# Six pairs of token groups loaded, scaled and scored with two tokens per partition, in a fused retention and gated two-layer kernel

## Chip, cores and metric

The kernel runs on one core of a Trainium2 chip. The metric is the device time of one execution in microseconds. Before the change the median of three runs is 299.77 us (299.62 to 301.11).

## What is computed

Eight batches of 576 tokens, eight heads of 64, give 4608 tokens of width 512. A masked linear attention with a decay per head comes first; a two-layer product with g = h cos(h) between the layers follows. Inputs and output are float32.

```
scores = (1/8) * q @ k.T                      # per batch and head, 576 x 576
Dmat   = where(i >= j, gamma[h] ** (i - j), 0)
attn   = (scores * Dmat) @ v
x      = attn with heads side by side          # 4608 x 512
h      = x @ w_in                              # 512 -> 2048
out    = (h * cos(h)) @ w_out                  # 2048 -> 512
```

## The kernel before

**Tiling.** The 4608 tokens are 36 groups of 128, numbered 0 to 35. Nine groups make two batches (`PER` = 9), and a group with g % 9 == 4 (`MIX`: 4, 13, 22, 31) lies across the end of a batch. The decay is split into a factor on q and a factor on k, so that each group needs only a 0/1 mask on its own 128 x 128 scores, and the earlier groups of the batch come in through a carried state of 64 x 64 per head.

**One group's way.** `load` (L105) brings q, k and v in with one DMA each from SP's queue, 128 partitions by 8 heads by 64 floats, in packets of 256 bytes (a token of one head). `prep` (L131) multiplies q and k by their factors into `qks` (L140, on GpSimd, 128 x 512 each) and rounds v to bfloat16 (L156). A group across two batches also copies the second batch's rows into `v_odd` (L158), whose other rows are zero, so that its state takes only these. `transposes` (L164) turns q and k: for groups below 6 on TensorE, with ScalarE copying the result (L177), from group 6 on by a DMA of SP's queue (L167). `scores` (L187) multiplies k by q (L195); VectorE masks the result (L207). `state` (L219, one group, L231) and `states` (L248, two groups, L266) make k.T @ v, and VectorE keeps the running sum (L285, L287) or masks it (L240). `attn_out` (L293) sums the group's own product, scores by v (L333), and the carried one, q by state (L319), and an engine moves it to `xT` (L350).

**Forms on TensorE.** The profile writes a matmul's place in the array as rows*columns. In `scores` with `parts=2` four matmuls of 64*64 use four quarters of the array; in `states` and the own product two matmuls of 128*64 use its two column halves; `attn_out` of two groups has its carried product in 64*64, with four quarters in turn.

**The two-layer part.** Tokens are taken in ten stretches n of widths 512, 256, 256 and seven times 512. `mm1` (L354) makes h (L365), ScalarE the cosine (L373), VectorE the product `gT` (L374). For n = 0 to 2, `mm2` (L376) makes the second product with 16 matmuls per 128 tokens (L382), ScalarE copies it (L392), SP stores it, and `feed(s)` follows. From n = 3 on, `mm2_seven` (L527) uses seven products of quarter matrices (L517) instead of eight; their sums of quarters of g (`g_sum`, L425, L445) are made by GpSimd and VectorE, the sums of quarters of w_out by `w_sums` (L404, L418).

**What sets the order.** The order is written by hand: each engine, and each DMA queue of SP or GpSimd, does its instructions in the order in which the Python program issues them, and waits at an instruction until its inputs are there. For n = 0 to 2, a list `todo` of (index, work) is mixed into the sequence of `mm2` matmuls: the work is issued ahead of the matmul with that index. For n = 0 the 64 matmuls run as `order` (L842 to L848): indices 0 to 31 are tokens 0 to 255, 32 to 47 the third 128 and 48 to 63 the fourth. `feed(s)` is called by `mm2` after the last matmul of each 128 tokens, so after indices 27, 31, 47 and 63. It issues loads, preps and transposes (L599 to L631). By its limits it issues, in this order:

| call | after index | issues |
|---|---|---|
| feed(0) | 27 | load 6, prep 6, load 7, transposes 6 |
| feed(1) | 31 | prep 7, load 8, prep 8, transposes 7, load 9, transposes 8 |
| feed(2) | 47 | prep 9, load 10, prep 10, transposes 9, load 11, transposes 10 |
| feed(3) | 63 | prep 11, load 12, prep 12, transposes 11, load 13, transposes 12 |

Groups 4 and 5 are loaded at L726 and L727, the first gated behind the second part of w_out, and prepared at L739, ahead of all that `feed` issues. Preps up to group 15 are issued in n = 0 to 2, the later ones by n = 3 and on.

Of the kernel before, what the change touches and what calls it, by code (L numbers as in the profile page):

```python
# [17 lines left out]
def kernel(  # L18
# [17 lines left out]
    P = 128  # L36
# [19 lines left out]
    N_PE_T = 6  # L56
    S7 = 3
# [27 lines left out]
    gk = consts.tile([P, PER, H], F32)  # L85
    ln_scale = consts.tile([P, 1], F32)
    half_pi = consts.tile([P, 1], F32)
    tri = consts.tile([P, P], F32)
    tri_mix = consts.tile([P, P], F32)
    diag2 = consts.tile([P, P], F32)  # L90
# [5 lines left out]
    v_odd = consts.tile([P, 2, H, D], BF16)  # L96

# [6 lines left out]

    def load(g, names="qkv", gate=None):  # L105

        t0 = g * P
# [4 lines left out]
        for name in names:  # L112
            src = {"q": q, "k": k, "v": v}[name]
            f = ld.tile([P, H, D], F32, tag="f" + name, name=f"f{name}")
            for p0, p1, t in parts:
                b, s0 = divmod(t, S)
                i = nc.sync.dma_start(  # L117
                    f[p0:p1], src[b, :, s0 : s0 + p1 - p0, :].rearrange("h s d -> s h d")
                )
                if gate is not None:  # L120
                    tc.add_manual_dep(
                        i.ins, gate.ins.name,
                        mybir.DependencyInfo(
                            mybir.DependencyClass.Sync, mybir.DependencyReason.DATA
                        ),
                        reason="weights first",
                    )
                    gate = None
            tiles["f" + name, g] = f

    def prep(g, early=False, kv_first=False):  # L131

        c = g % PER
# [30 lines left out]
    def transposes(g, banks=None, only=(0, 1)):  # L164
        qks, vb, qkT, qT = tiles["a", g]
# [52 lines left out]

    def state(g):  # L219
# [3 lines left out]
        qks, vb, qkT, qT = tiles["a", g]  # L223
# [4 lines left out]
        p0 = HP if c == g == MIX else 0  # L228
        vs = v_odd[:, g // PER % 2] if c == MIX and g > PER else vb
        for hg in range(HG):  # L230
            nc.tensor.matmul(  # L231
                ps[:, hg, :],
                lhsT=qks[p0:, 1, 2 * hg : 2 * hg + 2, :].rearrange("s h d -> s (h d)"),
                rhs=vs[p0:].rearrange("s (a b) d -> s b a d", a=2)[:, hg],
                start=(fresh and hg == 0),
                stop=(c in (MIX - 1, PER - 2) and hg == HG - 1),
                skip_group_check=True,
            )
# [9 lines left out]
    def states(gs, bank="st"):  # L248
# [6 lines left out]
        apart = bank == "b"  # L255
        if apart:
            two = psum.tile([P, 2, 2, HG, D], F32, tag=bank, name="st")
            ps = two[:, :, 0]
        else:
            ps = psum.tile([P, len(gs), HG, D], F32, tag=bank, name="st")  # L260
        for x, g in enumerate(gs):
            qks, vb, qkT, qT = tiles["a", g]
            vs = v_odd[:, g // PER % 2] if g % PER == MIX else vb
            for hg in range(HG):
                for he in range(2):
                    nc.tensor.matmul(  # L266
                        ps[he * D : he * D + D, x, hg, :],
                        lhsT=qks[:, 1, 2 * hg + he, :],
                        rhs=vs[:, head(he, hg), :],
                        start=((apart or x == 0) and hg == 0),  # L270
                        stop=((apart or x + 1 == len(gs)) and hg == HG - 1),
                        skip_group_check=True,
                    )

        def copy(run=nc.vector.tensor_copy):
            for g in gs:
                s, sb = tiles.pop(("s32", g)), blocks4[g % 4]
                run(sb, s)
                tiles["sb", g + 1] = sb

        def add():
            for x, g in enumerate(gs):
                s = stp.tile([P, HG, D], F32, tag="s32", name="s32")
                if g % PER in (0, MIX):
                    nc.vector.tensor_copy(s, ps[:, x])  # L285
                else:
                    nc.vector.tensor_tensor(out=s, in0=ps[:, x], in1=tiles["s32"], op=ALU.add)  # L287
# [361 lines left out]
    for p0, c0, c1, base in (  # L649
# [4 lines left out]
        )  # L654
    nc.gpsimd.memset(tri, 1.0)
# [23 lines left out]
    nc.scalar.activation(gk, pos, ACTF.Exp, bias=0.0, scale=-1.0)  # L679
    nc.vector.memset(v_odd[:HP], 0.0)  # L680
    nc.vector.memset(diag2, 0.0)
# [38 lines left out]
    for g in range(G4):  # L720
# [3 lines left out]
        if g == 2:  # L724
# [4 lines left out]
            nc.gpsimd.memset(tri_mix[:HP, HP:], 0.0)  # L729
        if g + 1 < G4:  # L730
# [8 lines left out]
    for g in (4, 5):  # L739
        prep(g)  # L740
# [3 lines left out]
    def pair(g, banks, sc, av):  # L744

        mid = (sc + av) // 2
        return [
            (sc - 5, lambda: state(g)),
            (sc, lambda: (scores(g, banks[0]), scores(g + 1, banks[1]))),
            (mid, lambda: state(g + 1)),  # L750
            (av, lambda: attn_out([g, g + 1], banks[0])),
        ]

    def scores2(g, put_off=None):
        if g < NG:
# [3 lines left out]
    def unit(g, bank, more=True, soon=False):  # L759

        attn_out([g, g + 1], bank, nc.scalar.copy)
        copy = states([g + 1, g + 2])()
# [7 lines left out]
    def unit7(g, bank, more=True, then=lambda: None, put_off=None):  # L770
# [3 lines left out]
        attn_out([g, g + 1], "m", nc.scalar.copy)  # L774
# [5 lines left out]
    for n, w in enumerate(widths):  # L780
# [6 lines left out]
        elif n == 1:  # L787
            blocks = [(et, half * P, P) for half in range(2) for et in (0, 8)]
# [6 lines left out]
        for i, (et, c0, cw) in enumerate(blocks):  # L795
# [3 lines left out]
                (1, 0): {4: lambda: scores(5, "a")},  # L799
                (1, 1): {3: lambda: attn_out([5], "a", evac=nc.scalar.copy)},  # L800
# [8 lines left out]
        if n == 0:  # L809
            todo = [  # L810
                (34 + 5 * i, lambda x=x, e=e: w_sums(x, e, e + 4))
                for i, (x, e) in enumerate((x, e) for x in (1, 6, 7) for e in (0, 4))
            ] + [
                (45, lambda: transposes(4, "ab")),
                (49, lambda: state(4)),
                (50, lambda: scores(4, "a")),
                (57, lambda: attn_out([4], "a")),
# [66 lines left out]
```

## Time and profile before

| | |
|---|---|
| median of three runs | 299.77 us |
| span of the profiled execution, first to last instruction | 298.2 us |
| TensorE busy | 287.1 us, 3113 matmuls |
| TensorE clock granted, mean | 1.000 |
| VectorE, ScalarE, GpSimd busy | 207.9, 135.9, 209.4 us |
| DMA packets, of these under 512 bytes | 154304, 140832 |
| DMA queue of SP (q1): packets, MB, share of 16 engines | 149504, 45.10, 77.2% |
| n = 0: first layer, second layer begin at | 17.91, 32.79 us |
| n = 1: first layer, second layer begin at | 49.17, 57.61 us |
| n = 2: first layer, second layer begin at | 67.49, 74.47 us |
| n = 3: first layer begins at | 84.18 us |

The span is what the profiler saw of one execution; the time of that execution itself is not among its rows, so the distance of 1.6 us from span to median is used for it. The beginnings are those of the first matmul of L365 or L382 in the order of time on TensorE.

A view in order of time gives start, length, engine, line and operation of each instruction or run of equal instructions, then the idle time ahead of it and what ended that. Matmuls overlap, so that the time from one start to the next is the cost and the length is not.

### The profile page before, as it was taken

Reading aid. Unit: us, or ns where it says so; the run is one execution under the profiler, and the core shown is the slowest. Engines: PE = TensorE matmul, PEld = TensorE weight load, DVE = VectorE, ACT = ScalarE, POOL = GpSimd, SP = SyncE. Lnnn points to the kernel's source line nnn. Section 1 sums busy time; section 2 is a strip of 40 time slices with the busy share of each in tenths; the row PEclk is TensorE's granted clock in tenths of the full one; section 3 lists DMA queues with packets and bytes.
Section 4 is the critical chain, followed back from the end, with each engine's and each line's share of the span. In section 5 each row is a group of like instructions: output and inputs, shape, how many; then the busy total and the mean of one; then the engine's idle time right before and its main releaser. Section 6 shows DMA issues by size and latency. Waiting matters only on the chain.

```text
span 298.2 us, 7384 instructions
## 1 busy us (share of the span) xinstructions
PE 287.1 (96%) x3113; PEld 195.3 (65%) x3113; DVE 207.9 (70%) x245; ACT 135.9 (46%) x167; POOL 209.4 (70%) x214
## 2 busy tenths in 40 slices
PE   8899999999999999979999999999999999999995
PEld 3478646848578786448744875488448845874584
DVE  5677637564579994788848874887489757935872
ACT  2656433514255432642346554546464446425620
POOL 2750066436445599997999999599959946980693
PEclk9999999999999999999999999999999999999999
DMA  7999999999999999999999997998690260031013
GB/s 203 212 209 206 209 214 213 200 243 208 208 174 222 211 239 213 217 279 176 198 224 229 209 200 183 212 208 201 122 194 2 73 143 0 2 106 36 0 44 99
DMA packets 154304, 50.28 MB, mean 169 GB/s; under 512 B 140832, under 2 KB 153248, under 8 KB 154272
## 3 DMA queue, kind: packets, MB, share of 16 engines
q1 hardware_dynamic: 149504, 45.10, 77.2%
q0 software_dynamic: 4224, 4.19, 8.5%
q8 instruction: 24, 0.39, 0.6%
q10 hardware_dynamic: 544, 0.52, 0.5%
q14 instruction: 8, 0.07, 0.1%
HBM read 36.70 MB, written 9.44 MB: 155 GB/s over the span
## 4 chain that ended last, share of the span: by engine, by line
PE 43%; POOL 25%; SPq 13%; DMA 8%; DVE 5%; issue 3%; ACT 1%; POOLq 0%; DVEq 0%
PE h L365 22%; POOL gs L445 17%; PE o L517 11%; SPq L117 8%; POOL qks L140 6%; PE o L382 5%; SPq L167 4%; DVE gT L374 3%; DMA fk<-in_k_dram 2%; DMA w_in_sb<-in_moe_w_in_dram 2%; DMA qkT<-qks 2%; POOL vb L156 2%; DVE gs L445 2%; DMA fv<-in_v_dram 1%; ACT cosh L373 1%
## 5 line engine op out<-in xcount | busy, mean ns | idle before, releaser
L445 POOL TENSOR_TENSOR gs<-gT 128x512 bf16<-128x512 bf16 x102 | 116.3, 1180 | 29.4 <-DVE gs L445 29.4
L365 PE MATMUL h<-xT,w_in_sb 128*128 128x512 bf16 (+2 forms) x832 | 127.6, 313 | 2.6 <-DVE gT L374 1.8
L374 DVE TENSOR_TENSOR gT<-h,cosh 128x1024 bf16<-128x1024 f32 x72 | 87.8, 1223 | 43.7 <-ACT cosh L373 40.7
L373 ACT ACTIVATE cosh<-h,half_pi 128x1024 f32<-128x1024 f32 x72 | 80.2, 1114 | 72.2 <-PE h L365 69.8
L365 PEld LDWEIGHTS <-w_in_sb 128*128 128x128 bf16 x832 | 75.9, 98 | 51.6 <-issue 3.0
L140 POOL TENSOR_TENSOR qks<-fq,gq 128x512 bf16<-128x512 f32 x32 | 34.0, 1062 | 40.9 <-DMA fq<-in_q_dram 40.9
L517 PEld LDWEIGHTS <-gs 128*128 128x128 bf16 x576 | 53.6, 98 | 10.1 <-POOL gs L445 2.9
L140 POOL TENSOR_TENSOR qks<-fk,gk 128x512 bf16<-128x512 f32 x35 | 37.3, 1066 | 8.0 <-DMA fk<-in_k_dram 7.4
L207 DVE TENSOR_TENSOR ret<-sc,tri 128x1024 bf16<-128x1024 f32 x32 | 38.1, 1217 | 2.8 <-PE sc L195 2.7
L517 PE MATMUL o<-ws,gs 128*128 128x256 bf16 (+1 forms) x352 | 39.1, 268 | 0.7 <-POOL gs L445 0.5
L382 PE MATMUL o<-w_out_sb,gT 128*128 128x512 bf16 x128 | 30.1, 380 | 0.0
L517 PE MATMUL o<-w_out_sb,gT 128*128 128x256 bf16 x224 | 26.6, 273 | 0.1
L517 PE MATMUL o<-w_out_sb,gs 128*128 128x256 bf16 x224 | 26.1, 273 | 0.5 <-POOL gs L445 0.4
L537 DVE TENSOR_TENSOR ot<-o,ot 128x512 f32<-128x512 f32 (+2 forms) x25 | 14.9, 603 | 14.7 <-PE o L517 14.5
L517 PEld LDWEIGHTS <-gT 128*128 128x128 bf16 x224 | 21.4, 98 | 4.7 <-DVE gT L374 0.7
L350 ACT CAST xT<-ov 128x1024 bf16<-128x1024 f32 (+1 forms) x18 | 16.5, 917 | 16.1 <-PE ov L319 13.9
L445 DVE TENSOR_TENSOR gs<-gT 128x1024 bf16<-128x1024 bf16 (+1 forms) x18 | 20.4, 1148 | 0.3
L382 PEld LDWEIGHTS <-gT 128*128 128x128 bf16 x128 | 11.8, 98 | 12.5
L156 POOL CAST vb<-fv 128x512 bf16<-128x512 f32 x22 | 14.3, 651 | 4.4 <-DMA fv<-in_v_dram 4.2
L564 ACT COPY ot<-o 128x512 f32<-128x512 f32 x7 | 4.1, 586 | 20.5 <-PE o L517 20.5
L392 ACT COPY ot<-o 128x512 f32<-128x512 f32 x8 | 4.7, 588 | 17.4 <-PE o L382 17.4
L537 DVE TENSOR_TENSOR ot<-ot,o 128x512 f32<-128x512 f32 x14 | 9.6, 684 | 4.0 <-ACT ot L569 2.4
(70 smaller groups left out, 175.8 us busy)
## 6 DMA issues: line engine op xcount, KB each, us to landing
out_dram<-ot SPq DMA_DIRECT2D x35, 256.0 KB, 4.0
fk<-in_k_dram SPq DMA_DIRECT2D x32, 256.0 KB, 5.2
fv<-in_v_dram SPq DMA_DIRECT2D x32, 256.0 KB, 5.2
fq<-in_q_dram SPq DMA_DIRECT2D x30, 256.0 KB, 4.5
w_in_sb<-in_moe_w_in_dram POOLq DMA_DIRECT2D x4, 512.0 KB, 8.9
w_out_sb<-in_moe_w_out_dram POOLq DMA_DIRECT2D x4, 512.0 KB, 16.2
fq<-in_q_dram SPq DMA_DIRECT2D x8, 128.0 KB, 4.0
fk<-in_k_dram SPq DMA_DIRECT2D x8, 128.0 KB, 4.4
```

The lines of the kernel that those rows point to most:

```text
L117: i = nc.sync.dma_start(f[p0:p1], src[b, :, s0 : s0 + p1 - p0, :].rearrange("h s d -> s h d"))
L140: eng.tensor_tensor(out=qks[:, m].rearrange("p (b a) d -> p a b d", a=2), in0=f.rearrange("p (a b) d -> p a b d", a=2), in1=by[:, c, :].re ...
L156: copy_v(vb, fv)
L207: nc.vector.tensor_tensor(out=ret.rearrange("p a b i -> p (a b) i"), in0=ps.rearrange("p a b i -> p (a b) i"), in1=mask.unsqueeze(1).to_br ...
L350: evac(tiles["x", n][:, :, t0 : t0 + len(gs) * P], ps.rearrange("p c x i -> p c (x i)"))
L365: nc.tensor.matmul(ps[:, j, :], lhsT=w_in_sb[:, dg, (et + j) * P : (et + j + 1) * P], rhs=xT[:, dg, c0 : c0 + w], start=(dg == 0), stop=(d ...
L373: nc.scalar.activation(cosh, ps, ACTF.Sin, bias=half_pi, scale=1.0)
L374: nc.vector.tensor_mul(gT[:, et : et + m, c0 : c0 + w], ps, cosh)
L382: nc.tensor.matmul(ps, lhsT=gT[:, et, tsi * P : (tsi + 1) * P], rhs=w_out_sb[:, et, :], start=(et == 0), stop=(et == ET - 1),)
L445: i = (nc.vector if on_dve else nc.gpsimd).tensor_tensor(out=tiles["gs", n, x][:, e : e + step], in0=i0, in1=i1, op=op_)
L517: nc.tensor.matmul(dst[i], lhsT=lhs[:, e, j * P : (j + 1) * P], rhs=rhs[:, e, c0:c1], start=(x in (3, 4, 1, 7) and e == 0 and (i == 0 or l ...
L537: pend.append(lambda: nc.vector.tensor_tensor(out=out_, in0=in0, in1=in1, op=op_))
```

## The change

Groups 4 to 15 become six pairs. A pair's 256 tokens lie two to a partition, the tokens 2i and 2i+1 of the pair in partition i, so that the first group has partitions 0 to 63 and the second 64 to 127. A tile of a load then holds four heads of 256 tokens (`he` is the half of the heads) in packets of 512 bytes. An even group's load brings q of both halves and k of the first, an odd group's brings k of the second and both halves of v. `prep2` does the same thirds on GpSimd. The DMAs and their sizes stay as many as before.

In the scores, own products and states, r (0 or 1) is the token in the partition, x the group in the pair. Of the own products and the states each matmul reads 64 partitions now instead of 128, and there are twice as many. The carried product reads all 128 partitions against a masked 128-column state `sb` instead of 64 against 64. New constants (`gq2`, `gk2`, three masks, `v2_odd`) are made by GpSimd, VectorE and ScalarE in the beginning.

Pair 2 (groups 4 and 5) has a way of its own: at the place of L739 only the first half of the heads of q and k is scaled on GpSimd. The rest is in the new `todo` of n = 0: VectorE scales the second halves at index 30, ScalarE rounds v and GpSimd copies the second batch's rows of v into `v2_odd` (`odd2`) at index 48, ahead of `state(4)` at index 54, whose matmuls read `v2_odd`. Group 5's scores and output, which stood in the first layer of n = 1, are now part of the pair; that layer runs in blocks of 256 tokens instead of 128.

The core of the diff:

```diff
+    PAIRED = range(4, 16)
...
+    def load2(g, gate=None):
...
+        for name, he in (("k", 1), ("v", 0), ("v", 1)) if g % 2 else (("q", 0), ("q", 1), ("k", 0)):
...
+            f = ld.tile([P, HG, 2, D], F32, tag="f" + name, name=f"f{name}")
+            for p0, p1, bb, sa in ((0, pm, b, s0), (pm, P, b + 1, 0)):
+                if p0 < p1:
+                    i = nc.sync.dma_start(
+                        f[p0:p1].rearrange("p h r d -> p h (r d)"),
+                        src[bb, he * HG : he * HG + HG, sa : sa + 2 * (p1 - p0), :].rearrange(
+                            "h (p r) d -> p h (r d)", r=2
+                        ),
+                    )
...
+    def rounded2(p, he, copy):
+
+        f = tiles["fv", p, he]
+        vb = nat.tile([P, HG, 2, D], BF16, tag="vb", name="vb")
+        copy(vb, f)
+        tiles["v2", p, he] = vb
+
+    def odd2(p, he, copy):
+
+        f = tiles.pop(("fv", p, he))
+        for x in mixed2(p):
+            r = slice(x * HP + QH, x * HP + HP)
+            copy(v2_odd[r, he * HG : he * HG + HG], f[r])
+
+    def prep2(g):
+
+        p = g // 2
+        if g % 2 == 0:
+            scaled2("q2", p, 0, nc.gpsimd)
+            scaled2("q2", p, 1, nc.gpsimd)
+            scaled2("k2", p, 0, nc.gpsimd)
+        else:
+            scaled2("k2", p, 1, nc.gpsimd)
+            for he in range(2):
+                rounded2(p, he, nc.gpsimd.tensor_copy)
+                odd2(p, he, nc.gpsimd.tensor_copy)
...
+    def scores_pair(g, banks="ab", put_off=None):
...
+        for r in range(2):
+            ps = psum.tile([P, 2, HG, P], F32, tag=banks[r], name="sc")
+            for hg in range(HG):
+                for x in range(2):
+                    i = slice(x * HP, x * HP + HP)
+                    for he in range(2):
+                        d = slice(he * D, he * D + D)
+                        nc.tensor.matmul(
+                            by_query(ps[i, he, hg, :]),
+                            lhsT=kT[d, r, hg, i],
+                            rhs=qT[d, :, hg, i],
...
+    def attn_pair(g, bank, evac=nc.scalar.copy):
...
+        def out_of(h, x):
+            return ps[h % 2 * D : h % 2 * D + D, x, h // 2, :]
...
+            for h0 in range(0, H, 2):
+                for r in range(2):
+                    for h in (h0, h0 + 1):
+                        for x in range(2):
+                            i = slice(x * HP, x * HP + HP)
+                            nc.tensor.matmul(
+                                out_of(h, x),
+                                lhsT=tiles["v2", p, h // HG][i, h % HG, r, :],
+                                rhs=ret[r][i, h // HG, h % HG, :],
...
+            for hg in range(HG):
+                for he in range(2):
+                    for x in range(2):
...
+                        nc.tensor.matmul(
+                            by_query(out_of(head(he, hg), x), n),
+                            lhsT=tiles["sb", g + x][:, hg, he * D : he * D + D],
+                            rhs=tiles["qT", p][:, :, hg, x * HP : x * HP + n // 2],
...
     def state(g):
...
+            for r, (kn, v_of) in enumerate(operands(g)):
+                for he in (0, 1) if g in PAIRED else (slice(0, 2),):
...
+                        lhsT=kn[:, 2 * hg : 2 * hg + 2, :].rearrange("s h d -> s (h d)"),
+                        rhs=v_of(he, hg),
...
     def states(gs, bank=("st",)):
...
+                for r, (kn, v_of) in enumerate(operands(g)):
+                    for he in range(2):
+                        nc.tensor.matmul(
+                            of[x][he * D : he * D + D, hg, :],
+                            lhsT=kn[:, 2 * hg + he, :],
+                            rhs=v_of(he, hg),
...
+                if g + 1 in PAIRED:
+                    sb = stp.tile([P, HG, P], BF16, tag="sb", name="sb")
+                    nc.vector.tensor_tensor(
...
-    for g in (4, 5):
-        prep(g)
+    for m in ("q2", "k2"):
+        scaled2(m, 2, 0, nc.gpsimd)
     loaded = prepared = transposed = 6
...
-        elif n == 1:
-            blocks = [(et, half * P, P) for half in range(2) for et in (0, 8)]
...
-                (1, 0): {4: lambda: scores(5, "a")},
-                (1, 1): {3: lambda: attn_out([5], "a", evac=nc.scalar.copy)},
+                (1, 0): {2: lambda: state(5)},
...
             todo = [
-                (34 + 5 * i, lambda x=x, e=e: w_sums(x, e, e + 4))
-                for i, (x, e) in enumerate((x, e) for x in (1, 6, 7) for e in (0, 4))
+                (18 + 3 * i, lambda x=x, e=e: w_sums(x, e, e + 4))
+                for i, (x, e) in enumerate((x, e) for x in (1, 6) for e in (0, 4))
             ] + [
-                (45, lambda: transposes(4, "ab")),
-                (49, lambda: state(4)),
-                (50, lambda: scores(4, "a")),
-                (57, lambda: attn_out([4], "a")),
-                (61, lambda: transposes(5, "ba")),
-                (63, lambda: state(5)),
+                (30, lambda: (scaled2("q2", 2, 1, nc.vector), scaled2("k2", 2, 1, nc.vector))),
+                (39, lambda: transposes2(4, "b")),
+                (44, lambda: transposes2(5, "a")),
+                (48, lambda: (scores_pair(4), [(rounded2(2, he, nc.scalar.copy), odd2(2, he, nc.gpsimd.tensor_copy)) for he in range(2)])),
+                (54, lambda: state(4)),
+                (61, lambda: attn_pair(4, "a")),
             ]
         elif n == 1:
-            todo = pair(6, "ab", 16, 27)
+            todo = pair(6, 8, 20) + [(4 * i, lambda e=4 * i: w_sums(7, e, e + 4)) for i in range(2)]
         elif n == 2:
-            todo = [(11, lambda: scores2(g)), (25, lambda: unit(g, "m", soon=True))]
-            late += [lambda: unit(g + 2, "b", False)]
+            todo = [(11, lambda: scores2(g)), (25, lambda: unit(g, "m", soon=True, st="b"))]
+            late += [lambda: unit(g + 2, "b", False, st=("st", "n"))]
```

`transposes2` is `transposes` for a pair's q (even group) or k (odd group), on TensorE for pair 2 and by DMA for the others. `pair` issues `state`, `scores_pair`, `state` and `attn_pair`, the last with ScalarE as the one that moves the result to `xT`, where VectorE did so before.

## The prediction

> **What bounds the kernel now.** I read the busy times first, then the waits, then the order of time on TensorE (PE), GpSimd (POOL) and SP.
>
> ```profile
> PE 287.1 (96%) x3113; PEld 195.3 (65%) x3113; DVE 207.9 (70%) x245; ACT 135.9 (46%) x167; POOL 209.4 (70%) x214
> POOL qks L140 <- DMA fq<-in_q_dram: 40.9, 12, 19.4
> PE h L365 <- DVE gT L374: 1.8, 1, 1.8
> PE h L365 <- DVE xT L350: 0.7, 1, 0.7
> ```
>
> The first line is the page's; the others are waits: engine, line, what it waits for, us in total, times, longest. PE is busy all through; behind the start its longest waits are 1.8 and 0.7 us. GpSimd waits 40.9 us for q, which costs nothing, since nothing that PE needs soon stands behind it. So a load that comes sooner wins little, and a thing that makes PE wait costs its whole length.
>
> ```profile
> 42.58 1.04 POOL L140 TENSOR_TENSOR qks<-fq,gq 128x512 bf16<-128x512 f32 x1 [0.33 <-DMA fq<-in_q_dram]
> 47.14 1.04 POOL L140 TENSOR_TENSOR qks<-fq,gq 128x512 bf16<-128x512 f32 x1 [1.79 <-DMA fq<-in_q_dram]
> ...
> 61.61 1.05 POOL L140 TENSOR_TENSOR qks<-fq,gq 128x512 bf16<-128x512 f32 x1 [1.70 <-DMA fq<-in_q_dram]
> 62.72 1.04 POOL L140 TENSOR_TENSOR qks<-fk,gk 128x512 bf16<-128x512 f32 x1
> ...
> 67.77 1.04 POOL L140 TENSOR_TENSOR qks<-fq,gq 128x512 bf16<-128x512 f32 x1 [3.24 <-DMA fq<-in_q_dram]
> 68.83 1.04 POOL L140 TENSOR_TENSOR qks<-fk,gk 128x512 bf16<-128x512 f32 x1
> ```
>
> These are preps in order of time (start, length, engine, line; in brackets the idle time before and its end): 42.58 is group 5, 47.14 group 6, 61.61 group 9 and 67.77 group 10. GpSimd takes them in the order of `feed` and stands still at each until its load has landed, though `feed` issued prep 10 behind index 47, which PE passed at about 44.
>
> **The step that decides: odd2.** At index 48 the change issues `odd2` of pair 2 on GpSimd. By the table of `feed`, preps 6 to 10 are issued ahead of it. `state(4)` at index 54 reads `v2_odd`, and all later matmuls stand behind it. So PE waits until GpSimd has done prep 10.
>
> When PE gets there: the second layer of n = 0 begins at 32.79; 54 matmuls of 512 columns at 0.216 (45 in the 9.71 from 32.79 to the first transposes) are 11.66; two sets of transposes as now, 0.44 each, 0.88; scores 0.58; and about 0.4 for ScalarE's copy of the second set (two copies of L177 take 1.07, the four matmuls between give 0.86). Sum 46.3.
>
> When GpSimd gets there: now the k of group 10 is multiplied from 68.83 on. What smaller packet numbers win: SP's queue (q1) takes 77.2% of 16 engines for 298.2 us over 149504 packets, 24.6 ns for 302 bytes on average; q10 takes 0.5% over 544, 44 ns for 956. On the line between, 256 bytes take 23.2 ns and 512 take 30.8. A group's load falls from 3072 x 23.2 / 16 = 4.45 us of all engines to 1536 x 30.8 / 16 = 2.96. The DMA shares from 40 to 70 us add up to 1.04 to 1.25 of the engines, so I count 1.25 us a group. Between the landing at 38.7 and 68.8 there are 6.3 loads (two thirds of 4 and 10, all of 5 to 9): 7.9 us. Load 10's three thirds are down by 60.9, scaled by 62.0, and two `odd2` copies, 0.65 each (L158 takes 0.61 at best for 64x512), end at 63.3. PE goes on at 63.4: **17.1 us of standing still**. Bounds: if a packet of 512 bytes costs two of 256, GpSimd ends at 71.3, and the wait is 25.0; if loads cost nothing, GpSimd's own work from 38.7 binds, thirteen multiplications at 1.04 and four roundings at 0.61, 16.0, and the two copies' 1.3: the wait is 9.7.
>
> **The clock after the wait.**
>
> ```profile
> 1.26 5.32 PE L185 MATMUL idle<-zeros 128*128 128x512 bf16 x14 [1.26 <-DVE zeros L662]
> 6.42 1.04 PE L708 MATMUL tr<-ident,qs 128*128 128x128 bf16 x8
> ```
>
> The first 14 matmuls of 512 columns, which follow on idleness, take 5.16 us to the next start; 14 x 0.216 is 3.0. Starting from rest costs 2.1 us. No PE wait in this trace is long enough to show whether a wait in the middle costs that too; after the 1.78 us one, eight matmuls of 512 take 1.72, full speed. Bounds 0 to 2.1; I take 2.1, as 17 us of rest is nearer to the start than to 1.8. The Trainium skill ("TensorE: Matmul & The Clock Gate", What's actually happening) says that the clock halves after at least one idle window of about 3.4 us and stays so for about 3.4 us of work, which would make 1.7 instead.
>
> **Matmuls.** Rows, from start to start:
>
> ```profile
> 87.77 0.64 PE L333 MATMUL ov<-ret,vb 128*64 128x128 bf16 x16
> 88.33 0.42 PE L319 MATMUL ov<-qkT,sb 64*64 64x128 bf16 x16
> 88.68 0.44 PE L266 MATMUL st<-vb,qks 128*64 128x64 bf16 x16
> 89.06 10.65 PE L365 MATMUL h<-xT,w_in_sb 128*128 128x256 bf16 x96
> ```
>
> Own 0.56, carried 0.35, two states 0.38. Between forms about 0.09 is lost; without it the own product is eight rounds of two column halves at 0.058, the carried four rounds of four quarters, the states eight rounds at 0.034.
> - Scores of a pair: 32 matmuls of 64*64 as now (32 in the 0.58 from 76.94 to 77.52). No change.
> - Own: twice as many, four quarters at a time, eight rounds. No change. Bounds: 0 to +0.45 if rows do not pair. Against this speaks the Trainium skill (same page, Back-to-back issue gap): no start follows another in under about 25 ns. The scores row shows 18 ns each, so here the measurement decides; by the rule 32 would take 0.8 and six pairs 2 us more.
> - Carried: 128*64, and the four that follow each other go to the same column half. Only each fourth overlaps: (16 - 3) x 0.056 = 0.73 instead of 0.23, +0.5 a pair; bounds 0 and +0.67 (all in line).
> - `states`: 16 a group, all in one row half: eight rounds at 0.034, +0.135 a group; bounds 0 and +0.27.
> - `state(g)`: 16 of 64*128, 64 columns: 16 x 0.034 and a change, 0.6 instead of 0.22; bounds 0 and +0.8.
>
> **The sum on PE.** From 63.4 on: `state(4)` 0.6, ten matmuls 2.16, output of pair 2 1.2 (own 0.45, carried with half a group at half width 0.5, changes 0.27), clock 2.1. The output stands three matmuls (0.65) ahead of n = 1, and ScalarE's move to xT takes 1.01: PE waits 0.5. n = 1 begins at 70.0 instead of 49.17: **+20.8**. Its first layer: 64 matmuls as in n = 2 (67.49 to 74.47, 6.98) and `state(5)` 0.6 against 8.44: -0.85. Its second: states +0.76, output 1.45 against 0.92, and the wait of 0.7 for xT goes, since ScalarE now has twelve matmuls of cover: +0.6. n = 2: carried for one group +0.17, states +0.27. The units of pairs 10, 12 and 14, in n = 3: carried +0.5, +0.35, +0.5, states +0.27, +0.27, +0.14: with the changes +2.05. n = 4: the 1.8 us wait, VectorE's sum (3.33 us at 126.30) while GpSimd prepares until 128.5: PE comes later against GpSimd by then, -1.2 (bounds 0, -1.8). Total 20.8 - 0.85 + 0.6 + 0.45 + 2.05 - 1.2 = 21.9.
>
> At nothing I cost: GpSimd's masks and positions and two more exponentials (GpSimd waits 19.35 before 38.68 and 5.18 before 7.72, ScalarE 3.6 before 7.49); VectorE's two multiplications at index 30 (0.69 each; its next due work is the masking at 45); six maskings of `sb`, 0.68 each, which go from ScalarE's 0.41 to VectorE (busy 13.4 of 15.4 us in the first layer of n = 3; without cover +0.7 each). SP's stores and loads behind load 11 wait for the third store of n = 0, as now at 72.91; PE gets there near 69, so they are not later.
>
> Span 298.2 + 21.9 = 320.1, and the 1.6 from span to median: **321.6 us**.
>
> **Rivals.** (a) `odd2` isn't what PE waits for, because it gets ahead of the preps. Then the wait and the clock's 2.1 go, and n = 1 begins at 50.8: 1.6 - 0.85 + 0.6 + 0.45 + 2.05 - 1.2 = 2.65, 302.4. For it: all rows of v that `odd2` needs are down by 44. Against: each GpSimd row above stands in the order of issue, also behind a load that isn't there. (b) Not slower: the sooner loads take PE's waits away, 1.78 at 130.8, 0.69 at 67.5 and the small ones for GpSimd and VectorE (0.45, 0.46, 0.27), 3.6 in all. It decides once `odd2` ends before 46.3 and the new matmuls overlap so that they add less than that; adding nothing gives 296.2, half 298. For it: the 40.9 us of waits for q. Against: they end on GpSimd, not PE. (c) The 512-byte packets win nothing: the wait of 25.0, 329.5.
>
> **Chances.** Forecast with its bounds, (c) among them, 0.83; (a) 0.08; about no change 0.04; (b) 0.05. A measurement tells 0.5% (1.5 us) from no change. Faster 0.05, same 0.04, slower 0.91. The bounds of the wait and of the clock span 312 to 330; 313 to 330 holds some 0.8.
>
> **What would show it.** Right: one PE gap from about 46 to 63 that ends with the copy into `v2_odd` on GpSimd, itself behind group 10's multiplications; the chain of waits running through SP and GpSimd there; slow matmuls behind it; carried products of 128*64 near 0.73. Wrong: that copy before 46, PE without a gap over 2 us, or group 10 prepared by 55.

## The result, and the profile after

The changed kernel takes **328.95 us** (median of four runs, 328.51 to 329.37), the kernel before, beside it on the same chip, 300.44 us (299.62 to 303.84). The ratio is 1.094, 95% interval 1.087 to 1.100: slower by 28.5 us. The forecast was 321.6 with a range from 313 to 330. Medians and ranges, here and below, are of all runs; the ratios leave out those in which the chip was in a slower state.

Busy times, two of the rows of 40 slices, and SP's queue, from the page:

```profile
PE 290.4 (89%) x3257; PEld 198.3 (61%) x3281; DVE 208.3 (64%) x249; ACT 139.8 (43%) x168; POOL 213.2 (65%) x233
PE   7899970048999899999998999999999999999995
PEclk9999996558999999999999999999999999999999
q1 hardware_dynamic: 131264, 45.10, 65.0%
```

PE's busy time grew by 3.3 us alone, the span from 298.2 to 327.3. The seventh and eighth slices hold most of the difference: PE does nothing there, and the granted clock falls with it. SP's queue brought the same 45.10 MB in fewer packets, and its share of 16 engines fell from 77.2% to 65.0%, of a longer span. The loads, though, did not stay as many as before: 118 DMAs of SP's queue became 130, since pair 4 (groups 8 and 9) lies across a batch's end and takes twelve DMAs of 128 KB where the two groups took six of 256, and pairs 2 and 6 take twelve instead of nine.

GpSimd in order of time (the profile calls the tile `v2_odd` by the name `v_odd`, and line 170 is `odd2`), then PE:

```profile
59.42 1.04 POOL L148 TENSOR_TENSOR k<-fk,gk 128x512 bf16<-128x512 f32 x1 [1.78 <-DMA fk<-in_k_dram]
...
65.20 2.04 POOL L148 TENSOR_TENSOR q<-fq,gq 128x512 bf16<-128x512 f32 x2 [2.78 <-DMA fq<-in_q_dram]
67.20 1.04 POOL L148 TENSOR_TENSOR k<-fk,gk 128x512 bf16<-128x512 f32 x1
68.31 1.16 POOL L170 CAST v_odd<-fv 32x512 bf16<-32x512 f32 x2
```

```profile
45.78 1.47 PE L607 MATMUL o<-w_out_sb,gT 128*128 128x512 bf16 x6
68.96 0.21 PE L442 MATMUL st<-v_odd,k 64*128 64x64 bf16 x1 [21.71 <-POOL v_odd L170]
69.52 0.95 PE L442 MATMUL st<-v_odd,k 64*128 64x64 bf16 x15 [0.35 <-POOL v_odd L170]
70.81 2.77 PE L607 MATMUL o<-w_out_sb,gT 128*128 128x512 bf16 x6 [0.34 <-issue]
```

One gap of 21.7 us ends with `odd2`'s first copy, and that copy directly follows group 10's multiplications (65.20 to 68.24), as the order of issue has it. The six matmuls of 512 columns behind it take 2.69 us to the next start (73.50), 0.45 each with the change of form, instead of 0.216.

The chain that ended last, between 48 and 70 us (start, us, what):

```profile
50.50 3.28 DMA fq<-in_q_dram
...
53.94 1.05 POOL q L148
54.99 0.17 SPq L192
...
55.21 0.60 SPq L132
...
55.86 3.43 DMA fk<-in_k_dram
...
59.42 1.05 POOL k L148
60.48 0.07 SPq L192
...
61.28 3.79 DMA fq<-in_q_dram
...
65.20 1.79 POOL q L148 x2
```

This is a circle through three queues: a load lands, GpSimd scales it, SP's transpose of that group (L192), which had waited for the scaling, lets the next load (L132) go, and that takes 3.3 to 3.8 us to land. The windows of the two kernels show what it does to the transfers (start and end, us; then the engines' busy times, granted clock, DMA share, which is the time of all packets by that of 16 engines and passes 1 where packets overlap, and GB/s). Before:

```profile
33.00:48.00 15.00, 15.00 (x100) 7.12 (x99) 7.76 (x11) 3.85 (x6) 6.67 (x7) 1.00 1.21 212
48.00:58.00 10.00, 9.99 (x170) 8.87 (x168) 5.93 (x6) 5.79 (x8) 5.60 (x7) 1.00 1.23 223
```

After:

```profile
33.00:48.00 15.00, 13.90 (x107) 7.04 (x107) 8.99 (x10) 5.95 (x9) 5.41 (x5) 1.00 1.20 260
48.00:58.00 10.00, 0.00 (x0) 0.00 (x0) 0.50 (x1) 0.00 (x0) 5.73 (x7) 0.69 0.88 192
```

Up to 48 us the larger packets win: 260 GB/s instead of 212 at the same share. Behind it the rate falls to 192, below that of before, with a share of 0.88 instead of 1.23: the queue now waits.

Where the 29.1 us of span came from, in us, by the beginnings of the stages on PE:

| stretch | before | after | difference |
|---|---|---|---|
| up to the second layer of n = 0 | 32.79 | 33.55 | +0.76 |
| second layer of n = 0 | 16.38 | 43.22 | +26.84 |
| n = 1, first and second layer | 8.44, 9.88 | 8.74, 10.47 | +0.30, +0.59 |
| n = 2 | 16.69 | 17.55 | +0.86 |
| n = 3 | 32.60 | 34.01 | +1.41 |
| n = 4 | 33.05 | 31.70 | -1.35 |
| the rest | 148.37 | 148.06 | -0.31 |

### The profile page after: what moved, and what is told of

Same layout as the page of the kernel before. It is cut to its first block, busy times and chain, and to the rows that moved or that the text cites. A ratio compares the mean times of both kernels' runs of the same rounds, so it can differ in the third digit from the quotient of the medians.

```text
span 327.3 us, 7749 instructions
## 1 busy us (share of the span) xinstructions
PE 290.4 (89%) x3257; PEld 198.3 (61%) x3281; DVE 208.3 (64%) x249; ACT 139.8 (43%) x168; POOL 213.2 (65%) x233
## 2 busy tenths in 40 slices
DMA packets 136065, 50.30 MB, mean 154 GB/s; under 512 B 104160, under 2 KB 135008, under 8 KB 136032
## 3 DMA queue, kind: packets, MB, share of 16 engines
q1 hardware_dynamic: 131264, 45.10, 65.0%
## 4 chain that ended last, share of the span: by engine, by line
PE 44%; POOL 29%; DMA 10%; issue 6%; DVE 5%; ACT 2%; SPq 2%; POOLq 0%; DVEq 0%
PE h L590 23%; POOL gs L670 19%; PE o L742 10%; POOL qks L330 6%; PE o L607 6%; DMA fq<-in_q_dram 5%; DMA fk<-in_k_dram 3%; DMA w_in_sb<-in_moe_w_in_dram 2%; DVE gT L599 2%; POOL vb L346 2%; POOL q L148 1%; ACT cosh L598 1%; POOL k L148 1%; PE ov L259 1%; ACT xT L293 1%
## 5 line engine op out<-in xcount | busy, mean ns | idle before, releaser
L590 PE MATMUL h<-xT,w_in_sb 128*128 128x256 bf16 (+1 forms) x756 | 126.6, 325 | 3.1 <-ACT xT L293 1.1
L148 POOL TENSOR_TENSOR q<-fq,gq 128x512 bf16<-128x512 f32 x11 | 11.8, 1085 | 40.0 <-DMA fq<-in_q_dram 29.9
L330 POOL TENSOR_TENSOR qks<-fk,gk 128x512 bf16<-128x512 f32 x23 | 24.0, 1045 | 5.0 <-DMA fk<-in_k_dram 5.0
L400 DVE TENSOR_TENSOR ret<-sc,tri 128x1024 bf16<-128x1024 f32 x22 | 26.3, 1216 | 0.9 <-PE sc L388 0.9
L451 DVE TENSOR_TENSOR sb<-st,diag 128x512 bf16<-128x512 f32 x8 | 5.5, 685 | 30.5 <-PE st L442 29.2
L293 ACT CAST xT<-ov 128x1024 bf16<-128x1024 f32 x6 | 7.8, 1305 | 38.4 <-PE ov L276 38.4
L330 POOL TENSOR_TENSOR qks<-fq,gq 128x512 bf16<-128x512 f32 x20 | 21.8, 1090 | 0.1
L442 PE MATMUL st<-v_odd,k 64*128 64x64 bf16 x16 | 1.2, 233 | 22.1 <-POOL v_odd L170 22.1
L670 DVE TENSOR_TENSOR gs<-gT 128x1024 bf16<-128x1024 bf16 (+1 forms) x18 | 17.3, 977 | 0.3
L442 PEld LDWEIGHTS <-k 64*128 64x128 bf16 x64 | 2.5, 101 | 23.6 <-issue 23.6
```

The costliest lines, as they stand in the source:

```text
L148: eng.tensor_tensor(out=tiles[m, p].rearrange("p r (b a) d -> p a r b d", a=2)[:, he], in0=tiles.pop(("f" + m[0], p, he)).rearrange("p b r ...
L293: evac(tiles["x", n][:, :, t0 : t0 + 2 * P].rearrange("p c (x i r) -> p x c r i", x=2, r=2), ps.rearrange("p x c (r i) -> p x c r i", r=2),)
L330: eng.tensor_tensor(out=qks[:, m].rearrange("p (b a) d -> p a b d", a=2), in0=f.rearrange("p (a b) d -> p a b d", a=2), in1=by[:, c, :].re ...
L400: nc.vector.tensor_tensor(out=ret.rearrange("p a b i -> p (a b) i"), in0=ps.rearrange("p a b i -> p (a b) i"), in1=mask.unsqueeze(1).to_br ...
L590: nc.tensor.matmul(ps[:, j, :], lhsT=w_in_sb[:, dg, (et + j) * P : (et + j + 1) * P], rhs=xT[:, dg, c0 : c0 + w], start=(dg == 0), stop=(d ...
L670: i = (nc.vector if on_dve else nc.gpsimd).tensor_tensor(out=tiles["gs", n, x][:, e : e + step], in0=i0, in1=i1, op=op_)
```

## The experiments

Theory: the place of `odd2` behind `feed`'s preps costs the whole gap and the clock; the new forms of the matmuls cost a little. Rivals: the gap has another cause (transposes, scores, rounding), or the pairing itself is what is slow.

**odd2 ahead of feed(0).** The two copies are issued at index 26 of n = 0 instead of 48, and nothing else changes.

```diff
+                (26, lambda: [odd2(2, he, nc.gpsimd.tensor_copy) for he in range(2)]),
...
-                (48, lambda: (scores_pair(4), [(rounded2(2, he, nc.scalar.copy), odd2(2, he, nc.gpsimd.tensor_copy)) for he in range(2)])),
+                (48, lambda: (scores_pair(4), [rounded2(2, he, nc.scalar.copy) for he in range(2)])),
```

> The kernel after the change, with one step moved: GpSimd's two copies into v_odd of pair 2 are issued ahead of the first feed (index 26) instead of behind the third (index 48); engine and work are the same. Theory (the order on GpSimd makes the gap): the 22.1 us in which TensorE stands still go, and with them about 3 us of half clock, so 328.95 - 25.1 = about 304 us (302.5 to 305.5), and no TensorE gap over 2 us between 40 and 80. Rival (the rows of v or other loads come late themselves, whatever the order): most of the gap stays, over 315 us. The prediction's own rival (a) priced a kernel without the gap at 302.4.

Measured: 304.16 us (303.59 to 308.74), ratio 1.012 (1.008 to 1.017). GpSimd, then PE:

```profile
43.18 1.23 POOL L170 CAST v_odd<-fv 32x512 bf16<-32x512 f32 x2 [1.34 <-DMA fv<-in_v_dram]
```

```profile
45.11 1.47 PE L607 MATMUL o<-w_out_sb,gT 128*128 128x512 bf16 x6
46.51 0.64 PE L442 MATMUL st<-v_odd,k 64*128 64x64 bf16 x16
```

The copies are done at 44.4, the states follow the matmuls without a gap, and the mean clock is 1.000. Two instructions of 0.6 us in the wrong place of one queue cost 24.8 of the 28.5 us. What is left is 3.7 us (3.5 against the kernel before beside it, 300.63).

**Warm matmuls in the gap.** The changed kernel with 100 idle matmuls of 512 columns ahead of `state(4)`; the gap stays.

```diff
-                (54, lambda: state(4)),
+                (54, lambda: (warm(psum.tile([P, 512], F32, tag="n", name="idle"), 100), state(4))),
```

> The kernel after the change, with 100 matmuls of zeros (512 columns, into a free bank, 21.3 us at full clock) issued ahead of state(4), so that TensorE works through the time in which it stood still; nothing else changes. Theory (the low clock behind the gap is an own cost of about 3 us): granted clock 1.0 from 47 us on, the matmuls behind state(4) run at 216 ns per 512 columns instead of 427, and 325.5 to 326.5 us. Rival (the low clock costs nothing that counts, since later waits take it up): 328.5 to 329.5 us.

Measured: 326.34 us (325.76 to 327.05), ratio 1.087 (1.083 to 1.091).

```profile
69.95 0.59 PE L442 MATMUL st<-v_odd,k 64*128 64x64 bf16 x15 [0.37 <-POOL v_odd L170]
70.48 1.68 PE L607 MATMUL o<-w_out_sb,gT 128*128 128x512 bf16 x7
```

Now the seven matmuls take 1.61 to the next start (72.09), full speed. From the 15 states to the beginning of n = 1 it is 4.67 us (69.95 to 74.62) against 7.25 (69.52 to 76.77): the clock costs **2.6 us**, in the trace as in the median.

**Loads one group further ahead.** Is it SP's order of issue, as the circle says, that keeps group 10 back? `feed` lets one more load go ahead of each transpose.

```diff
-                transposed <= loaded - 2 or loaded == NG or (s > 3 and loaded == before)
+                transposed <= loaded - 3 or loaded == NG or (s > 3 and loaded == before)
...
-            elif loaded < min(NG, 2 * s + 8, s + 13):
+            elif loaded < min(NG, 2 * s + 9, s + 13):
```

> The kernel after the change, with feed issuing one more load ahead of each transpose (limit loaded - 3 instead of loaded - 2, and one load more per call); the copies into v_odd stay behind prep 10. Theory (behind 48 us the loads come slowly because each stands behind a transpose in SP's queue that waits for GpSimd, not because a packet of 512 bytes is dear): prep 10 ends near 60 instead of 68.2, the gap shrinks by 5 to 8 us, 321 to 324 us. Rival (the packets or the DMA engines set the pace): gap and time as they were, 328 to 329.5 us.

Measured: 325.69 us (325.40 to 327.54), ratio 1.086 (1.081 to 1.091). GpSimd, then PE:

```profile
63.98 1.04 POOL L148 TENSOR_TENSOR k<-fk,gk 128x512 bf16<-128x512 f32 x1 [0.24 <-DMA fk<-in_k_dram]
```

```profile
65.74 0.21 PE L442 MATMUL st<-v_odd,k 64*128 64x64 bf16 x1 [18.78 <-POOL v_odd L170]
```

Group 10's k is scaled at 63.98 instead of 67.20, and PE waits 18.78 instead of 21.71 us. The direction is that of the theory, the size about half of it.

**The carried product in another order.** The first experiment's kernel, with the heads of the two column halves in turn. The two matmuls of a head (one per group) still follow each other in the same half, so that two in one half follow two in the other, where four followed four. It tests the price that the prediction gave to four in one half: by that price seven of the sixteen would overlap instead of three, some 0.2 us less a pair and over 1 in all.

```diff
-            for hg in range(HG):
-                for he in range(2):
+            for he, hg in [(he, h0 + j) for h0 in (0, 2) for he in range(2) for j in range(2)]:
+                if True:
```

> e1_odd_first with the carried product's matmuls reordered, so that each two that follow each other go to different column halves. The prediction's price (four in the same half follow one another, 0.73 us for 16): 0.2 to 0.3 us a pair less than e1_odd_first, 1.0 to 1.5 us in all. Rival (what the trace of the changed kernel shows, 16 in about 0.5 us without the change of form, so that they overlap already): within 0.3 us of e1_odd_first.

Measured: 303.58 us (303.47 to 309.50), ratio 1.011 (1.007 to 1.015), where without the new order the ratio was 1.012 (1.008 to 1.017). A carried product takes 0.57 from start to start:

```profile
97.72 0.64 PE L276 MATMUL ov<-qT,sb 128*64 128x128 bf16 x16
98.29 0.60 PE L480 MATMUL st<-vb,k 64*64 64x64 bf16 x32
```

The price was wrong. The changed kernel's own trace says why, at full clock:

```profile
117.12 0.64 PE L259 MATMUL ov<-ret,vb 64*64 64x128 bf16 x32
117.69 0.66 PE L276 MATMUL ov<-qT,sb 128*64 128x128 bf16 x16
118.28 0.59 PE L480 MATMUL st<-vb,k 64*64 64x64 bf16 x32
118.81 0.28 PE L590 MATMUL h<-xT,w_in_sb 128*128 128x256 bf16 x1
```

From start to start the own product takes 0.57, the carried 0.59 and the states of two groups 0.53. Sixteen matmuls of 128 columns in 0.50 (0.59 less the change of form) are 31 ns each, so two already share the time of one (0.058) although they stand in the same column half. The trace has the first ten of them start in twos, 13 or 14 ns apart and then 42 to 66, and each two are the two groups of one head, so in one half.

**Two small waits taken away.** The first experiment's kernel with two edits.

```diff
-        banks = {0: "abmabmab", 1: "bmba", 2: "bmab", 3: "mamabmab"}.get(n, "abmabmab")
+        banks = {0: "abmabmab", 1: "bmab", 2: "bmab", 3: "mamabmab"}.get(n, "abmabmab")
...
-                (61, lambda: attn_pair(4, "a")),
+                (58, lambda: attn_pair(4, "a")),
```

> The kernel with odd2 moved to index 26, and two waits of its trace taken away: the banks of n=1's first layer in the order b, m, a, b instead of b, m, b, a (its trace shows PE waiting 0.72 us for VectorE's gT at 56.27 us, before the third block, which asks for bank b again), and attn_pair(4) at index 58 instead of 61 (PE waited 0.64 us at 51.23 us for ScalarE's xT). Theory (what is left of the loss beside the one long gap is a row of small waits, each worth its own length): 304.2 - 0.7 - 0.6 = 302.8, between 302.4 and 303.2, and the two stages shorter by these amounts. Rival (the waits only move to the next block or the next product, since VectorE and ScalarE are as late there): 303.7 to 304.4.

Measured: 302.17 us (301.77 to 302.42), ratio 1.007 (1.005 to 1.010), beside 299.98 for the kernel before. Both waits are gone, and beside the kernel before what is left fell from 3.53 to 2.19 us; n = 1's first layer takes 7.87 us (50.30 to 58.17) where the first experiment's took 8.53 (51.23 to 59.76). So the waits (0.72 and 0.64 us) were worth their length, 1.34 us, as the theory had it; its range from 302.4 lay a little too high.

**The kernel before, one copy moved from VectorE to ScalarE.** Would the waits of the kernel before be worth as much to it?

```diff
-            (av, lambda: attn_out([g, g + 1], banks[0])),
+            (av, lambda: attn_out([g, g + 1], banks[0], nc.scalar.copy)),
```

> The kernel before, with one edit: pair 6's outputs are copied out of PSUM by ScalarE instead of VectorE. In the trace of before PE waited 0.69 us at 67.49 us for this copy, which stood on VectorE behind a mask and a product while ScalarE had nothing to do. If the wait is all that ties the stage: 300.4 - 0.6 = 299.8, n=2's first layer 0.6 us earlier. Rival: ScalarE's copy of the same tile is bound by its own wait (the last product of the pair) and saves under 0.2: 300.2 to 300.5.

Measured: 302.44 us, spread from 298.70 to 304.30 over twelve runs; ratio 1.004 (1.001 to 1.007). No gain: both ideas missed. The wait of 0.69 for xT is gone from the trace, and this one is there instead, which before's trace doesn't have:

```profile
83.42 0.42 PE L195 MATMUL sc<-qkT 64*64 64x128 bf16 x16 [1.95 <-DMA qkT<-qks]
```

PE now waits for a transpose by DMA in n = 2. A copy that ends sooner brings PE to the next thing that is due, and that comes at its own time. Why it came as late as 83.4 here, and why the runs spread, wasn't settled.

**The same, and five casts on ScalarE.**

```diff
-            copy_v = nc.scalar.copy if g > starts[S7] // P + 17 else nc.gpsimd.tensor_copy
+            copy_v = nc.scalar.copy if g > starts[S7] // P + 17 or 17 <= g <= 21 else nc.gpsimd.tensor_copy
```

> The same, and the v casts of groups 17 to 21 on ScalarE, which takes five times 0.60 us from GpSimd's run of work between 111.5 and 129.1 us in the trace of before. There VectorE's sum of gT at 126.30 us took 3.33 us and ended 0.5 us behind GpSimd's last cast; PE waited 1.8 us behind it. Theory (VectorE's sum is held up while GpSimd works without a pause, and is let go when it stops): the sum ends about 2.5 us sooner or takes 0.7 us, the wait of 1.8 us is gone, 299.8 - 1.8 = 298.0 (297.6 to 298.6). Rival (the sum's length has another cause): it stays at 3.3 us, 299.4 to 300.2. This also tells whether the prediction's reason for n=4 (GpSimd against PE) was right.

Measured: 310.40 us (308.50 to 311.27), ratio 1.033 (1.029 to 1.036). A miss by 12 us, and by the very thing studied here. ScalarE, then PE:

```profile
126.17 0.62 ACT L156 CAST vb<-fv 128x512 bf16<-128x512 f32 x1 [5.88 <-DMA fv<-in_v_dram]
129.55 0.62 ACT L156 CAST vb<-fv 128x512 bf16<-128x512 f32 x1 [2.77 <-DMA fv<-in_v_dram]
130.07 2.11 ACT L373 ACTIVATE cosh<-h,half_pi 128x1024 f32<-128x1024 f32 x2
```

```profile
132.56 7.75 PE L365 MATMUL h<-xT,w_in_sb 128*128 128x512 bf16 x23 [7.04 <-DVE gT L374]
```

The casts of groups 20 and 21 waited for their loads, n = 4's cosines stood behind them in ScalarE's queue, and PE stood still for 7.0 us. The granted clock was 0.50 twice in this trace: for 10.2 us from 127.7 on, around the end of that wait, and for 3.4 us from 83.3 on, behind a wait of only 1.68 us for a transpose by DMA. There six matmuls take 2.56 us to the next start (86.70):

```profile
84.14 2.74 PE L382 MATMUL o<-w_out_sb,gT 128*128 128x512 bf16 x6 [0.33 <-issue]
```

In the trace of the experiment before this one the same six take 1.30 behind a wait of 1.95.

**Two tiles for xT in n = 3.** The kernel of the two small waits, with n = 3's halves of xT apart.

```diff
+        if n == 3:
+            tiles["x", n, t0] = xT = xp.tile([P, DG, 512], BF16, tag="xT", name="xT")
+            t0 = 0
...
-        gT, xT = tiles["g", n], tiles["x", n]
+        gT, xT = tiles["g", n], tiles["x", n, c0] if n == 3 else tiles["x", n]
```

> The kernel of the tidied waits, with one edit: n=3's two halves of xT lie in two tiles instead of one. Its trace shows PE stopping at 91.47 us, one matmul into the third block of n=3's first layer, for 0.66 us until ScalarE has written pair 10's outputs, although this block reads pair 8's columns alone; in the kernel before, whose write has plain columns, PE runs on there. Theory (the write with its two tokens strided apart is taken as one range over the whole tile from its first byte to its last, so it also stands ahead of a reader of the other half): the wait is gone, 302.2 - 0.65 = 301.5 (301.2 to 301.8). Rival (the block waits for ScalarE for another reason, the PSUM bank or its cosine): the wait stays, 302.0 to 302.4.

Measured: 301.47 us (301.06 to 303.33), ratio 1.006 (1.004 to 1.008). The wait is gone: the block runs on in one piece.

```profile
91.01 0.59 PE L485 MATMUL st<-vb,k 64*64 64x64 bf16 x32
91.53 3.67 PE L596 MATMUL h<-xT,w_in_sb 128*128 128x256 bf16 x32
```

In one tile, the write with its tokens strided apart had made a reader of the other half wait. This is the pairing's best version here, 1.4 us behind the kernel before (300.04 beside it).

**The kernel before, three casts on ScalarE.** Only those that had waited for no load.

```diff
-            copy_v = nc.scalar.copy if g > starts[S7] // P + 17 else nc.gpsimd.tensor_copy
+            copy_v = nc.scalar.copy if g > starts[S7] // P + 17 or 17 <= g <= 19 else nc.gpsimd.tensor_copy
```

> The kernel before, with one edit: the v casts of groups 17 to 19 on ScalarE. With the casts of 17 to 21 there, the casts of 20 and 21 stood on ScalarE ahead of the cosines and waited 5.88 and 2.77 us for their loads; those of 17 to 19 waited for nothing. GpSimd's run of work then ends 1.8 us sooner, near 127.3 us instead of 129.07. Theory (VectorE's sum, issued at 126.3 us, is held until GpSimd pauses): it ends near 127.9 instead of 129.6, and PE's wait of 1.78 us shrinks to 0 to 0.3: 299.98 - 1.6 = 298.4 (298.0 to 298.9). Rival (the sum's 3.33 us do not hang on the end of GpSimd's run): 299.7 to 300.3.

Measured: 298.85 us (297.74 to 302.07), beside 300.04; ratio 0.998 (0.995 to 1.001), so a gain of 1.2 us by the medians that the interval doesn't secure. VectorE's sum takes 1.44 instead of 3.33 us, and PE's wait of 1.78 is gone. But GpSimd's run of work ended at 129.28, no sooner than in the kernel before (129.07), as a load came late, so its end isn't what let the sum go. The theory's number came true and its reason didn't.

**Loads two groups further ahead.** As the third experiment, with `loaded - 4` and `2 * s + 10`.

> The changed kernel with its loads two groups further ahead of the transposes on SP instead of one further. With one further, group 10's loads were issued from 58.4 us on, behind two transposes and a store of 3.9 us together, and its k was scaled at 65.0 us. With these behind it too, theory (what is ahead on SP sets when group 10 comes down): its loads go out near 54.5 us, its k is scaled near 61.5, PE's gap ends near 62.5 instead of 66, and the time falls by another 3 to 3.5 us, 322 to 323. Rival (behind the transposes the transfers or GpSimd's own work set the pace: from group 6 on it has 13 multiplications of about 1.03 us and eight copies of 0.61 us ahead, some 18 us, and starts at 45.5): under 1 us more, 325 to 326.

Measured: 325.57 us (323.84 to 326.65), ratio 1.085 (1.080 to 1.090): the rival's number. Group 10's k is scaled 1.3 us sooner than with one group further (62.68), not 3.5, and PE's wait is 1.8 us shorter.

```profile
64.44 0.21 PE L442 MATMUL st<-v_odd,k 64*128 64x64 bf16 x1 [16.95 <-POOL v_odd L170]
...
157.26 1.89 PE L590 MATMUL h<-xT,w_in_sb 128*128 128x512 bf16 x8 [1.76 <-DVE gT L599]
```

n = 1 begins at 72.06, 4.7 us sooner than in the changed kernel (76.77) and 1.15 sooner than with one group further (73.21). But 1.8 us are given back in n = 4, where PE again waits for a sum on VectorE that takes 3.31 us; with one group further it didn't. Load 10 went out at 57.14, not near 54.5, and SP shows what stood ahead of it:

```profile
45.48 3.76 SPq L132 DMA_DIRECT2D fq<-in_q_dram  x4
49.34 2.92 SPq L132 DMA_DIRECT2D fk<-in_k_dram  x4
52.35 2.61 SPq L132 DMA_DIRECT2D fv<-in_v_dram  x4
55.01 1.33 SPq L192 DMA_TRANSPOSE qT<-q  x1
```

These are pair 4's twelve loads. SP is at them for 9.5 us (45.48 to 54.96), where the six of groups 8 and 9 in the kernel before take 2.4 and 2.2.

## Why the prediction was right, and where its sizes were off

**The deciding step was right.** PE stops at `state(4)`, until `odd2` has come through GpSimd behind prep 10. The gap began at 47.25 us (68.96 less 21.71; 46.3 forecast), ended with that copy, and moving the copy alone gave back 24.8 us.

**Mis-sized: the sooner loads.** They were to bring group 10's k forward by 7.9 us; it was scaled 1.6 us sooner (67.20 against 68.83). So the gap was 22.1 us with its second wait instead of 17.1, and these 5.0 us are most of the 7.35 that the forecast missed. The other large pieces are n = 1's first layer (1.15, below) and the beginning, put at nothing, which lost 0.76: there PE waits 0.64 us for w_in's first part, which it does not in the kernel before, and for 0 to 2.10 in the other traces of the pairing. The packets did win, and about what was priced: the time of SP's queue fell from 77.2% of 298.2 us to 65.0% of 327.3, by 17.5 us of all engines over twelve groups, 1.46 a group where 4.45 less 2.96 was said. But the step took the DMA shares of before, 1.04 to 1.25, as a bound that would stay. Once the transfers were shorter, the bound was the circle of SP's order. With two more loads let ahead the k was scaled at 62.68: the order held back 4.5 us. Of the last 1.8 us about one is GpSimd's, which in a pair scales two tiles of q ahead of the k: from group 10's first multiplication to its k it is 2.0 to 2.2 us (65.20 to 67.20, and 60.47 to 62.68) where it was 1.06. The cause of the rest stays open. The DMA engines are nearly full again there (share 0.98 from 48 to 58 us) at 198 GB/s, and pair 4's twelve loads, which cross a batch's end in pieces of 128 KB, keep SP for 9.5 us; a kernel without that crossing wasn't tried.

**Nearly right: the clock.** 2.1 us forecast from the start of the kernel, 2.6 measured. The granted clock was 0.50 from 51.9 to 75.8 us, of which 6.3 lie behind the beginning of work at 69.5. The Trainium skill ("TensorE: Matmul & The Clock Gate", What's actually happening) speaks of at least one busy window of about 3.4 us; the prediction worked out 1.7 from one such window, and the measurement is longer.

**Mis-sized: the carried product.** +0.5 a pair forecast, +0.24 measured (0.59 against 0.35), since two matmuls of one column half overlap. Own (0.57 against 0.56) and scores came out as said, states cost +0.15 for two groups instead of +0.27, and `state(g)` takes 0.57 (77.73 to 78.30) where 0.6 was said. So n = 3 lost 1.41 instead of 2.05, of which 0.65 was a wait that the prediction didn't see, the strided write of xT.

**Wrong: n = 1's first layer.** Forecast -0.85, measured +0.30. The step counted matmuls and missed that the banks of PSUM are asked for in the order b, m, b, a, so the third block waits 0.71 us for VectorE. With another order and the earlier output of pair 2 the layer takes 7.87, 0.57 less than before. The second layer (+0.6 forecast, +0.59) was right. n = 2 lost 0.86 instead of 0.45: scores wait 0.78 us for VectorE's sums of the states.

**Right in size, wrong in reason: n = 4.** The wait of 1.8 us went (-1.35 in all, -1.2 forecast), but not because PE came later against GpSimd. In the changed kernel the sum begins at 157.05 and takes 0.76 us while GpSimd has three more instructions of preparation to do. In the kernel before, and in the changed one with two more loads ahead, it takes 3.3 us with GpSimd at the same point, 0.2 us from the end of a cast and three instructions from a pause (before, then after):

```profile
126.30 3.33 DVE L445 TENSOR_TENSOR gs<-gT 128x1024 bf16<-128x1024 bf16 x1
```

```profile
157.05 0.76 DVE L670 TENSOR_TENSOR gs<-gT 128x1024 bf16<-128x1024 bf16 x1
```

The Trainium skill ("SBUF — State Buffer", SBUF: two separate sides) says that VectorE with two inputs in SBUF and a GpSimd instruction that reads SBUF exclude each other from a shared pair of ports for a whole instruction, whichever begins first. The traces agree that one holds the other up (in the changed kernel a multiplication of GpSimd takes 1.49 instead of 1.03 at the sum), but a wait over three instructions is more than that sentence says. What decides who gets in stays open, so these 1.8 us belong to neither kernel.

**The rivals.** (a) is the first experiment's kernel: 304.16 where 302.4 was worked out, the difference being of the size of small waits (0.72, 0.64, 0.66; a part of the second was in the sum) that only a trace of the new order shows. (b) isn't borne out by the version without these waits either, which is still 1.4 us behind. (c) had the nearest total, 329.5, for a reason that doesn't hold, since the packets did win. There was luck in the range: the result lies 1 us below its upper end, which was drawn for (c), and most of what used up that room was the order on SP's queue, which the prediction did not reckon with.

## What to carry to other kernels

A queue in order turns any wait of its head into a wait of all that is behind it: before an instruction goes to GpSimd or ScalarE, list what is issued ahead of it and which load each of these waits for, and look for the engine that needs its result first. A saving in transfer time is worth only what the order of issue lets through, so ask what is the bound once the transfers are shorter. And a small wait taken away is kept only if the next thing due is there: of the waits removed here, those in the pairing's kernel were kept whole, the one of 0.69 us in the kernel before wasn't, and that of 1.78 there gave 1.2 by the medians, which the interval doesn't secure.

## What the runs showed of the hardware

- After 22 us of rest TensorE started matmuls of 512 columns 0.43 us apart at first instead of 0.216, and the granted clock was 0.50 for 6.3 us from the beginning of work on; with idle matmuls in the gap there was no such stretch.
- Between the first and the last matmuls the traces have the clock at 0.50 for 3.41 and 10.24 us (five casts on ScalarE), 6.83 (the carried product in another order), 20.48 (loads further ahead, both) and 23.89 (the changed kernel): one, three, two, six and seven times 3.41. A wait of 1.68 us was followed by one of these stretches, waits of 1.78 and 1.95 by none.
- Two matmuls of 128*64 in the same column half, one behind the other, took the time of one: 16 of 128 columns in 0.50 us.
- From 33 to 48 us, with most loads in packets of 512 bytes, all transfers ran at 260 GB/s; with packets of 256 bytes at 212, at a DMA share of 1.20 and 1.21.
- A sum on VectorE of 128x1024 bfloat16 took 0.69 us with GpSimd idle, and 0.76 or 3.3 us with GpSimd at work at the same point of its run.
